# Spreading two rows with GpSimd instead of TensorE, zero matmuls among the first transposes, and a reordered end of the first stage in a fused RWKV-5 and SiLU kernel

## The chip, the cores and the metric

The kernel runs on one core of one Trainium2 chip. The metric is the device time of one launch, in microseconds (us); the figure quoted for a kernel is the median of several runs. Every time below comes from those runs or from one execution taken by the hardware profiler.

The engines are called as in the profile: PE is TensorE's matmul row and PEld its weight loads, DVE is VectorE, ACT is ScalarE, POOL is GpSimd, SP is SyncE. DMA transfers are issued from the queues of SP, ACT and POOL.

## The reference

A linear attention with a decaying state is followed by a two-layer network with SiLU. There are 4 batches, 8 heads, 768 time steps and a head size of 48; the second part has 3072 tokens of width 384 and a hidden width of 2048. All inputs and the output are float32.

```python
for t in range(S):
    cur = np.einsum('bhd,bhe->bhde', u[None] * kt, vt)
    y[:, :, t] = np.einsum('bhd,bhde->bhe', rt, state + cur)
    state = w[None, :, :, None] * state + np.einsum('bhd,bhe->bhde', kt, vt)
x = y.transpose(0, 2, 1, 3).reshape(B * S, H * D)
h = x @ w_in
out = (h * (1.0 / (1.0 + np.exp(-h)))) @ w_out
```

Here kt, vt and rt are the rows of k, v and r at time t; w (8 by 48) is the decay of each head and channel, and u (8 by 48) is the bonus factor of the present step.

## The kernel before

**Tiling.** The 768 steps are cut into 6 chunks of 128 steps. A unit is one chunk of one batch, so there are 24 units, numbered so that units 0 to 3 are the first chunk of the four batches, 4 to 7 the second, and so on. Four units of one chunk make a tile of 512 tokens for the network.

**One unit.** Three loads bring r, k and v of the unit into `rin`, `kin` and `vin` (line 71, 192 KB each). TensorE transposes r and k (`turn_one`, line 244, and `turn_ring`, line 254); DVE multiplies the transposes by powers of w into `rT` and `kT` (`decay_one`, line 260). For two units at a time 64 small float32 matmuls form the products of k and r (`product_pair`, line 283); DVE masks them (`masked`, line 300), and ACT casts v (`cast_v`, line 236, with two more copies that swap halves for odd units) and, from unit 4 on, r (`cast_r`, line 279). `outputs_y` (line 305) multiplies the masked products by v, and from the second chunk on adds the state's part. The bonus is made apart: POOL forms k times u (`bonus_ku`, line 209), then times r (`bonus_rku`, line 213), DVE sums over each head (`bonus_sum`, line 222), POOL multiplies v by the sum (`bonus_v`, line 227). For units 0 to 3 a matmul adds that to y in PSUM (`add_bonus`, line 321). POOL also forms k times its decay to the chunk's end (`decayed_k`, line 218), which `outputs_s` (line 325) uses for the state. y goes through a transpose into `xT`, the network's input.

**The network.** `l1` (lines 401 to 419) is a piece of the first layer: six matmuls for two of the 16 hidden tiles, then a SiLU on ACT. `l2` (line 451) and, for the first tile, `front_mm` (line 426) are pieces of the second layer. The first tile accumulates its second layer in the two `att` PSUM tiles, which the attention uses too, and `front_store` (line 431) copies it out of there on ACT.

**Order.** The schedule is by hand: each engine and each queue runs its instructions in the order in which the program issues them. After the constants (lines 97 to 138) a string of words named `order` (line 515) is walked word by word and covers units 0 to 7. A word names a step and a unit: Tr0 and Tk0 are the transposes of r and k of unit 0, rT0 and kT0 their products with powers of w, A01 a pair's products, am0 a mask, Y0, V0 and S0 the matmuls of `outputs_y`, `add_bonus` and `outputs_s`, ku0, ru0, rd0 and vu0 the four bonus steps, kc0 the decayed k, v160 and r164 the casts, y160 and yT0 the way of y into xT0. lr1, lk1 and lv1 are loads, issued on SP. q0 to q3 and o0 to o3 are loads of the network's weights, issued on POOL. L and G are first-layer matmuls and their SiLU for the first tile, M2.3 is the last of the four pieces of batch 2 in the second layer, osb2 its copy and store, H0 a whole piece of the next tile's first layer. hold6 is a memset on POOL (line 152) that writes a part of `rin` of unit 6, so that the load lr6 can't start ahead of it. clear writes zeros into the `att` tiles by six matmuls of a zero operand (`zeros`, line 155). Then a loop (line 547) takes two units at a time from unit 6 on, and between its attention steps calls `fill`, which takes pieces of the network off a list.

**The two rows.** w and u are loaded as one row each on one partition. They are needed on all 128 partitions: u for ku, and the logarithm of w for `lamC`, which the kc steps use. A matmul with a column of ones does that (`spread_row`, line 178): word ub for u, copied from PSUM to `u_bc` on DVE by ubc, and word wb for w, from which ACT takes the logarithm at once (`ln_w`, line 185).

```python
def spread_row(name, row):
    spread[name] = ps.tile([128, HD], FP, name="bc", tag="moe", bufs=4)
    nc.tensor.matmul(spread[name], ones, row, start=True, stop=True)
```

## Time and profile before

| What | Value |
|---|---|
| Median of 3 runs | 196.67 us (196.13 to 197.16) |
| The profiled execution's own time | 195.64 us |
| Its span in the profile | 193.8 us |
| Around the span | 1.84 us |
| Mean granted TensorE clock | 0.974 |
| Busy: PE, PEld, DVE, ACT, POOL | 186.7, 142.5, 102.1, 110.1, 120.6 us |
| Read from and written to HBM | 20.45 and 4.72 MB |

The span runs from the first to the last instruction that the profiler recorded. A share of busy time is a mean over stages with different limits, so the page is read by stage: constants and first loads (to about 8 us), the attention of units 0 to 3 (to about 25), the string's remaining words (to about 53), and then a loop that repeats every 14.3 us.

### The profile page before, as it was taken

How to read it: one execution, taken by the hardware profiler on the slowest of the kernel's cores; microseconds unless marked ns; L12 is line 12 of the kernel's file. 1: busy time of each engine (PE TensorE's matmuls, PEld its weight loads, DVE VectorE, ACT ScalarE, POOL GpSimd, SP SyncE). 2: the span in 40 equal slices, each digit the busy share in tenths (PEclk: the TensorE clock that was granted, in tenths of full speed). 3: DMA queues.
4: the chain of work that ended last, by engine and by line, in shares of the span. 5: the costliest groups of instructions: out<-in, count | busy, mean ns of one | idle time of the engine just before them, and what ended most of it. 6: DMA issues, size and time to landing. Idle time of an engine off the chain costs nothing.

```text
span 193.8 us, 5942 instructions
## 1 busy us (share of the span) xinstructions
PE 186.7 (96%) x2476; PEld 142.5 (74%) x2476; DVE 102.1 (53%) x193; ACT 110.1 (57%) x208; POOL 120.6 (62%) x160
## 2 busy tenths in 40 slices
PE   7799999999798999999999999999999999999994
PEld 2578689756597688688688697697697697796873
DVE  6767776640654645646546556456466365262110
ACT  5266877703468557557557567457558458462540
POOL 8895996975895496496496595595694680300000
PEclk9756999999999999999999999999999999999999
DMA  5999899919961761952762952942953941202202
GB/s 101 222 213 209 136 159 189 163 38 212 233 180 39 156 177 41 185 143 44 157 173 44 180 148 42 206 123 46 181 147 62 188 123 41 81 4 44 81 0 81
DMA packets 90126, 24.17 MB, mean 125 GB/s; under 512 B 83314, under 2 KB 90100, under 8 KB 90100
## 3 DMA queue, kind: packets, MB, share of 16 engines
q1 hardware_dynamic: 84992, 20.39, 47.7%
q0 software_dynamic: 3712, 3.15, 11.0%
q8 instruction: 19, 0.31, 0.7%
q10 hardware_dynamic: 1396, 0.27, 0.7%
q14 instruction: 7, 0.06, 0.1%
HBM read 20.45 MB, written 4.72 MB: 130 GB/s over the span
## 4 chain that ended last, share of the span: by engine, by line
PE 92%; DMA 2%; ACT 2%; DVE 1%; SPq 1%; issue 1%
PE hps L406 32%; PE ops L439 26%; PE att L293 10%; PE att L428 5%; PE att L251 5%; PE tr L258 3%; PE yp L318 3%; DMA kin<-in_k_dram 2%; PE yp L313 2%; PE sp L334 2%; PE ops L464 1%; PE yp L322 1%; SPq L73 1%; PE bc L180 1%; DVE am L300 1%; ACT gT L414 1%
## 5 line engine op out<-in xcount | busy, mean ns | idle before, releaser
L414 ACT ACTIVATE gT<-hps 128x512 f16<-128x512 f32 x96 | 56.4, 597 | 43.5 <-PE hps L406 41.1
L406 PE MATMUL hps<-xT,win 128*128 128x256 f16 (+1 forms) x564 | 70.0, 275 | 0.6 <-DVE y L353 0.5
L406 PEld LDWEIGHTS <-win 128*128 128x128 f16 x564 | 53.2, 98 | 9.2 <-issue 0.9
L439 PE MATMUL ops<-wout,gT 128*128 128x384 f16 x304 | 52.4, 326 | 0.0
L439 PEld LDWEIGHTS <-gT 128*128 128x128 f16 x304 | 29.1, 98 | 18.1
L229 POOL TENSOR_TENSOR vu<-vin,rku 128x384 f32<-128x384 f32 x24 | 19.7, 829 | 32.0 <-DVE rku L224 28.7
L300 DVE TENSOR_TENSOR am<-att,maskM 128x1024 f16<-128x1024 f32 x12 | 14.7, 1224 | 35.5 <-PE att L293 35.5
L211 POOL TENSOR_TENSOR ku<-kin,u_bc 128x384 f32<-128x384 f32 x24 | 24.1, 1007 | 3.8 <-DMA kin<-in_k_dram 3.8
L215 POOL TENSOR_TENSOR rku_f<-rin,ku 128x384 f32<-128x384 f32 x24 | 24.0, 1001 | 1.3
L219 POOL TENSOR_TENSOR kc<-kin,lamC 128x384 f16<-128x384 f32 x24 | 24.0, 1004 | 0.1
L293 PE MATMUL att<-rT,kT 48*64 48x128 f32 (+1 forms) x768 | 20.7, 257 | 1.1 <-ACT osb L445 1.1
L293 PEld LDWEIGHTS att<-rT,kT 48*64 48x64 f32 x768 | 18.7, 140 | 3.9 <-issue 1.7
L353 DVE TENSOR_TENSOR y<-yp,vu 128x384 f16<-128x384 f32 x20 | 11.2, 558 | 16.1 <-PE yp L318 5.4
L266 DVE TENSOR_TENSOR rT<-att,lamR 112x512 f32<-112x512 f32 x20 | 13.7, 686 | 9.3 <-PE att L251 9.3
L445 ACT COPY osb<-ops 128x384 f32<-128x384 f32 x16 | 7.7, 478 | 17.9 <-PE ops L439 17.9
L238 ACT CAST v<-vin 128x384 f16<-128x384 f32 x24 | 11.3, 509 | 6.3 <-DMA vin<-in_v_dram 6.2
L300 DVE TENSOR_TENSOR am<-att,maskX 128x1024 f16<-128x1024 f32 x12 | 14.6, 1216 | 0.0
L345 POOL TENSOR_TENSOR sdec<-st,wCT 112x384 f32<-112x384 f32 x16 | 13.2, 826 | 1.6 <-DVE st L368 1.5
L266 DVE TENSOR_TENSOR kT<-att,lamK 112x512 f32<-112x512 f32 x20 | 13.5, 681 | 0.0
L364 DVE TENSOR_TENSOR st<-sp,sdec 48x192 f32<-48x192 f32 x32 | 11.2, 351 | 2.6 <-POOL kc L219 1.6
L373 POOL CAST stb<-st 112x384 f16<-112x384 f32 x16 | 8.1, 505 | 7.3 <-DVE st L364 7.1
L281 ACT CAST rT<-rT 112x512 f16<-112x512 f32 x20 | 12.4, 620 | 0.2
(80 smaller groups left out, 198.2 us busy)
## 6 DMA issues: line engine op xcount, KB each, us to landing
rin<-in_r_dram SPq DMA_DIRECT2D x24, 192.0 KB, 3.6
vin<-in_v_dram SPq DMA_DIRECT2D x24, 192.0 KB, 3.6
kin<-in_k_dram SPq DMA_DIRECT2D x23, 192.0 KB, 3.5
out_dram<-osb SPq DMA_DIRECT2D x23, 192.0 KB, 3.0
win<-in_moe_w_in_dram POOLq DMA_DIRECT2D x4, 384.0 KB, 6.1
wout<-in_moe_w_out_dram POOLq DMA_DIRECT2D x4, 384.0 KB, 8.7
xT<-y SPq DMA_TRANSPOSE x18, 2.3
kin<-in_k_dram ACTq DMA_DIRECT2D x1, 192.0 KB, 3.6
```

The source lines that it names most:

```text
L211: nc.gpsimd.tensor_tensor(out=L(i)["ku"], in0=kin[i % NIN][:, :, 0:D], in1=u_bc, op=ALU.mult)
L215: nc.gpsimd.tensor_tensor(out=L(i)["rku_f"], in0=rin[i % NIN][:, :, 0:D], in1=L(i)["ku"], op=ALU.mult)
L219: nc.gpsimd.tensor_tensor(out=kc[i % NIN][:, :, 0:D], in0=kin[i % NIN][:, :, 0:D], in1=lamC, op=ALU.mult)
L229: nc.gpsimd.tensor_tensor(out=L(i)["vu"], in0=vin[i % NIN], in1=L(i)["rku"].unsqueeze(2).broadcast_to([128, H, D]), op=ALU.mult)
L266: nc.vector.tensor_tensor(out=L(i)[key].rearrange("p g (y t) -> p y g t", y=2), in0=L(i)["t"][0:PR, :, x], in1=lam.rearrange("p g (y t) -> ...
L281: nc.scalar.copy(out=L(i)["rT16"], in_=L(i)["rT"])
L293: nc.tensor.matmul(a[e][o0:o0 + HC, j, p, c0:C], kT[r0:r0 + D, p, s0:s0 + HC], rT[r0:r0 + D, p, c0:C], start=True, stop=True)
L300: nc.vector.tensor_tensor(out=am.rearrange("p h g c -> p (h g) c"), in0=L(i)["a"].rearrange("p h g c -> p (h g) c"), in1=(maskX if crossed ...
L345: nc.gpsimd.tensor_tensor(out=L(i)["sdec"], in0=st[b], in1=wCT.unsqueeze(2).broadcast_to([PR, NP, PW]), op=ALU.mult)
L406: nc.tensor.matmul(hps[:, f, :], win[:, q, (ft + f) * 128:(ft + f + 1) * 128], xts[sc][:, q, b0:b0 + nb, :].rearrange("p b t -> p (b t)"), ...
L414: nc.scalar.activation(out=gts[sc][:, ft:ft + m, b0 * C:(b0 + nb) * C], in_=hpss[b0, ft], func=AF.Silu)
L439: nc.tensor.matmul(opss[b], gts[sc][:, ft, b * C:(b + 1) * C], wout[:, ft, :], start=(ft == 0), stop=(ft == NFT - 1))
```

## The change

Four things are edited. Words and names are those of the section on the kernel.

- u and w are spread by GpSimd's partition_broadcast, from the one-partition row straight into SBUF: u among the constants, between the memsets of `st` and those of `rin` and `kin`; w by a new word wbc, between q0 and vu0. The two matmuls, the column of ones and the DVE copy are gone.
- Zero matmuls of 512 columns are added: clear has eight instead of six, three words z write to the `att` tile that the next pair of transposes does not use, and zs writes twice to a PSUM tile of its own just ahead of A01. The transposes of k of unit 0 go ahead of those of r of unit 1.
- For units 6 and 7 the casts v166, r166, v167 and r167, which stood in the loop's first pass, become words ahead of M2.3 and M3.3, the last second-layer pieces; osb2 and osb3 stand ahead of H0; a second piece H1 stands ahead of A67 and is taken off the loop's list.
- hold6 goes from after M0.1 to before Y4. The loads that follow change order: lv7 and lv6 come ahead of those of units 8 and 9.

```diff
     for b in range(B):
         nc.gpsimd.memset(st[b], 0.0)
+    nc.gpsimd.partition_broadcast(u_bc.rearrange("p h d -> p (h d)"), u_row)
     for i in range(B, NIN):
         nc.gpsimd.memset(rin[i][:, :, D:64], 0.0)
...
     def clear():
-        for n in range(6):
+        for n in range(8):
             zeros(att[n % 4 // 2][:, n % 2, :])
...
-    def spread_row(name, row):
-        spread[name] = ps.tile([128, HD], FP, name="bc", tag="moe", bufs=4)
-        nc.tensor.matmul(spread[name], ones, row, start=True, stop=True)
-
-    def copy_u():
-        nc.vector.tensor_copy(out=u_bc.rearrange("p h d -> p (h d)"), in_=spread["u"])
+    def spread_w():
+        nc.gpsimd.partition_broadcast(w_bc, w_row)
+
+    def zero_behind():
+        zeros(att[(len(turns) + 1) % 2][:, 0, :])
+
+    def zero_ring():
+        zs = ps.tile([128, 512], FP, name="zs", tag="moe", bufs=4)
+        for _ in range(2):
+            zeros(zs)
...
-        clear lr1 lk1 lk2 lnw lk3 eK ub lv0 lv1 lamK lr2 mx lr3 Tr0 ubc Tr1 lr5 rT0
-        Tk0 ku0 lv5 Tk1 rT1 lr4 ku1 kT0 Tk2 lv3 lv2 kT1 ru0 lk4 kT2 A01 ku2 lk5 rd0
-        lv4 kcm ru1 v161 wb q0 am0 Tr2 v160 vu0 lnwb am1 Y0 ku3 lamC Tk3 Tr3 rT2 ru2
+        clear lr1 lk1 lnw lk2 eK lk3 lv0 lv1 lamK lr2 mx lr3 Tr0 rT0 lr5 z z Tk0 kT0
+        ku0 lv5 z Tr1 Tk1 rT1 kT1 lr4 ku1 Tk2 lv3 lv2 ru0 lk4 kT2 zs A01 ku2 lk5 rd0
+        lv4 kcm ru1 v161 q0 wbc am0 Tr2 v160 vu0 lnwb am1 Y0 ku3 lamC Tk3 Tr3 rT2 ru2
...
-        sd4 L4.13 G4.12 am4 G0.10 L0.8 ku5 G4.13 L4.15 kc5 G0.8 Y4 S4 G4.15 M2.0 st4
-        ru5 Y5 M1.0 stb4 rd5 S5 sd5 M0.0 M2.1 vu4 st5 M3.0 stb5 y164 M0.1 hold6 vu5
-        lr6 M1.1 lk7 y165 L4.14 lk6 M1.2 G4.14 lr7 yT4 lk8 M1.3 lv7 M0.2 lk9 ku7 M0.3
-        lv6 M2.2 lv9 osb0 ku6 lv8 M2.3 lr8 ru7 yT5 Tr6 Tk6 xT5 lr9 xT4 kc6 M3.1 rT6
-        osb1 osb2 Tr7 Tk7 rd7 kT6 vu7 M3.2 rT7 ru6 M3.3 kT7 H0 osb3 rd6 A67
+        sd4 L4.13 G4.12 am4 G0.10 L0.8 ku5 G4.13 L4.15 kc5 hold6 G0.8 Y4 S4 G4.15 M2.0
+        st4 ru5 Y5 M1.0 stb4 rd5 S5 sd5 M0.0 M2.1 vu4 st5 M3.0 stb5 y164 M0.1 vu5 lr6
+        M1.1 lk7 y165 L4.14 lk6 M1.2 G4.14 lr7 yT4 xT4 M1.3 lv7 lv6 M0.2 ku7 lr8 lk8
+        lv8 lr9 lk9 lv9 M0.3 osb0 osb1 ku6 M2.2 ru7 yT5 xT5 Tr6 rT6 Tk6 kT6 kc6 v166
+        M3.1 r166 M3.2 v167 rd7 vu7 ru6 Tr7 rT7 Tk7 kT7 r167 M2.3 M3.3 osb2 osb3 H0
+        rd6 H1 A67
...
-    fillers.extend(first(1, 0, 2) + second(1, 0))
+    fillers.extend(first(1, 0, 4) + second(1, 0))
...
-        if i > B + 2:
-            fill(4)
-        else:
-            for n in (i, i + 1):
-                cast_v(n)
-                cast_r(n)
-                fill(2)
+        fill(4)
```

## The prediction

> **What bounds the kernel now.** I read the page's busy rows, then the chain that ended last.

> ```profile
> PE 186.7 (96%) x2476; PEld 142.5 (74%) x2476; DVE 102.1 (53%) x193; ACT 110.1 (57%) x208; POOL 120.6 (62%) x160
> PEclk9756999999999999999999999999999999999999
> PE 92%; DMA 2%; ACT 2%; DVE 1%; SPq 1%; issue 1%
> ```

> TensorE bounds the whole. Its matmuls carry 92% of the chain, so after the start a gain can only come from matmuls run sooner or faster. The clock row shows the weak place: slices 1 to 3 (4.8 to 19 us) are below full clock. By windows of 1 us it falls in the window 7 to 8 (0.68), is 0.50 from 8 on, and is full again by 18. The chain in order of time says what this costs, and where else PE stands still:

> ```profile
> 3.26 4.05 DMA kin<-in_k_dram
> 7.36 1.10 PE tr L258 x4
> 8.46 3.39 PE att L293 x62
> 11.85 1.57 PE bc L180 x2
> ...
> 16.86 1.08 PE yp L322 x2
> ...
> 18.30 1.52 PE att L293 x64
> ...
> 52.25 0.47 issue
> 52.72 0.48 ACT osb L445
> ```

> The same pair's products take 3.39 us at 8.46 and 1.52 at 18.30. The spreading of w (L180) is 1.57 on the chain. At 52.25 the products of units 6 and 7 wait 1.0 for ACT's copy out of `att`.

> Then GpSimd's own timeline at the start, since the change puts work there:

> ```profile
> 0.80 0.20 POOL masks.py:197 MEMSET ident<- 128x128 f32 x1 [0.29 <-POOLq L609]
> 1.08 0.29 POOL masks.py:199 TENSOR_SCALAR_AFFINE_SELECT ident<-ident 128x128 f32<-128x128 f32 x1
> ...
> 2.46 1.49 POOL L135 MEMSET st<- 112x384 f32 x4
> ...
> 5.73 1.01 POOL L211 TENSOR_TENSOR ku<-kin,u_bc 128x384 f32<-128x384 f32 x1 [0.61 <-DMA kin<-in_k_dram]
> ...
> 10.51 0.93 POOL L84 DMA_DIRECT2D win<-in_moe_w_in_dram  x1
> 11.46 0.84 POOL L229 TENSOR_TENSOR vu<-vin,rku 128x384 f32<-128x384 f32 x1
> ...
> 18.12 2.40 POOL L229 TENSOR_TENSOR vu<-vin,rku 128x384 f32<-128x384 f32 x3 [2.00 <-DVE rku L224]
> ```

> POOL is idle 0.61 us once between 0.8 and 16.1, and 2.0 after that. What is put into it there is delay for vu0 (11.46) almost in full; vu0 is what V0 (PE, 16.86) adds.

> [...]

> **The change part by part.**

> *Broadcasts.* [...] Removed: two PE records of u (0.91, ahead of transposes that wait for loads: 0), DVE's copy (0.56: 0), and w's 1.57 on the chain.

> [...] four real exchanges in POOL's order. No trace here prices one. [...] a gain is excluded, since each is an added step. [...]

> Queued behind them is all of POOL, then DVE's rd0 (waits for ru0) with kcm, am0 and am1 behind it, then PE's Y0 and V0 and all after, then ACT's y160. Durations from the trace:
> - [...]
> - ku0, ku1, ru0, ku2, ru1 at 0.96 each to 22.4; q0 0.93 to 23.4.
> - [...] vu0 ends 36.7.
> - ku3, ru2, ru3, kc0 at 0.96, vu1 and vu2 at 0.8: vu2 ends 42.2, against 19.8 now.

> V2 on PE then ends near 42.9 instead of 22.2: **+20.7**. POOL itself is 22.4 late, and has 1 to 2 us of lead over PE later on (kc3 ends 28.35, S2 needs it from 29.77; DVE waits 1.59 for kc5's issue near 38). It keeps about half of the difference: +21.5. PE stands idle before V0, so it restarts at half clock: [...] +2.

> *Zeros.* Two more in clear [...] end at 4.9 where Tr0 starts at 4.80; three z and two zs are 0.2 to 0.4 each, in PE's waits for loads (idle 5.2 to 5.96 and 7.05 to 7.36). Their gain, a clock that holds, would be 3.39 - 1.52 = 1.9 on A01 and about as much on what follows. Together with w's 1.57 it is worth nothing here, because vu0 sets V0. Moving Tk0 ahead of Tr1: 0, both wait for loads.

> *End of the string.* osb3 is out before A67, with H0 and H1 (0.66 each) over it: -1.0. Casts of units 6 and 7 leave ACT's line in the loop, where SiLUs stand behind them and PE waits: from A67 to the next transposes PE takes 53.25 to 62.19, 8.94 us, against 68.54 to 76.49, 7.95, in the next pass: -1.0. H1 only moves a piece: 0.

> *hold6, loads.* hold6's memset at 41.46 moves behind kc5 (37.8). SP has stood 23.0 us before it, so lr6 and the eleven loads behind it start up to 3.7 us earlier against their work. POOL's wait for kin (3.15 at 45.71) shrinks; worth 0, since PE's chain is solid from 32.08 to 52.25. If that cover went, o3 (issued 34.23, 8.7 to landing) would share the DMA with those loads; M0.3 needs it near 47, 4 us later.

> **Sum**: +21.5 + 2 - 2 = +21.5. The profiled execution took 195.64 (span 193.8 and 1.84 around it): 217.1. The median of before lies 1.03 above its profiled run, so I state **218**.

> **The rivals.**

> *A, exchanges that cost nothing to speak of* (the other side: faster). [...] T4 can't start before kin4 lands (16.43 + 3.7 = 20.1 against 22.16 now, -2.0). So -1.7 at the start and -2 at the end: 193. The clock need not hold for this: w's 1.57 goes either way. [...] It decides from 1.3 us for an exchange down: the shift at V2 is the four of them less 3.1 [...], and at 5.1 in all it only eats the end's 2.

> *B, dearer exchanges.* [...] 10 us each: 4 x 4.05 more, 234.

> *C, one trip.* The second pair is absent or cheap [...]: 11.9 less, 206.

> **How the numbers follow.** Main case 0.60, A 0.30, B 0.06, C 0.04. The main case alone, exchanges of 3.5 to 8.5 us, gives 208 to 228. A has 0.30, too much to leave out, so the range goes from 192 to 228; B, a third of the part of A (190 to 196) and little of the main case lie outside. A difference of 0.5% (1 us) is what a measurement here can tell from none. Faster 0.29 (A), same 0.03 (exchanges near 1.3 us), slower 0.68.

> **What would show it.** Right: gaps of about 6 us on POOL ahead of the first broadcast, ku0, the second broadcast and vu0; vu0 near 36, V2 near 43; PE idle with a half clock between 10 and 40; A67 without a wait for osb; the loop at 14.3 us a pass as now. Wrong: vu0 before 15 (A), or one pair of gaps (C). If A67 still waits, the -2 is lost. If vu0 is late and V2 isn't, my reading of who waits for POOL is wrong.

## The result, and the profile after

The changed kernel takes 220.95 us (median of 4 runs, 220.57 to 221.26), the kernel before 196.91 us (median of 4, 196.13 to 198.04). The ratio is 1.1215, with a 95% interval of 1.1155 to 1.1275: **slower by 24 us**. Ratios here and below leave out executions more than 1.5% above the fastest of the same kernel, so that a ratio and the quotient of two medians can differ a little. The profiled execution took 221.08 us, its span is 219.4.

First the page of the changed kernel: busy times, the granted clock in 40 slices, and the shares of the chain that ended last.

```profile
span 219.4 us, 5954 instructions
PE 187.9 (86%) x2479; PEld 142.7 (65%) x2479; DVE 101.6 (46%) x191; ACT 109.7 (50%) x208; POOL 122.3 (56%) x162
PEclk9995555559999999999999999999999999999999
PE 80%; issue 13%; POOL 3%; DMA 2%; ACT 0%; ACTq 0%; POOLq 0%
```

TensorE's busy time is nearly what it was, and it fills 86% of the span instead of 96%. What grew on the chain is "issue", from 1% to 13% of the span, some 28 us in which an engine waits for nothing that the profile shows. Which engine that is, and what waits behind it, is in the waits of the first 90 us (columns: who waited for whom, us in total, times, the longest).

```profile
DVE rku L226 <- POOL rku_f L217: 27.7, 4, 14.9
ACT lnw_bc L188 <- POOL w_bc L177: 20.1, 1, 20.1
...
PE yp L324 <- POOL vu L231: 14.2, 1, 14.2
...
PE yp L320 <- DVE am L302: 11.6, 1, 11.6
...
POOL w_bc L177 <- issue: 7.4, 1, 7.4
POOL ku L213 <- issue: 7.0, 1, 7.0
POOL vu L231 <- issue: 6.9, 1, 6.9
POOL u_bc L135 <- issue: 5.9, 1, 5.9
```

The last four rows are the cause and the first four what it does. GpSimd stands still four times, once ahead of each of its two broadcasts and once ahead of the first multiply behind each. Its timeline puts them in order; the idle time before an instruction stands in brackets.

```profile
2.73 1.50 POOL L134 MEMSET st<- 112x384 f32 x4
10.12 0.68 POOL L135 PARTITION_BROADCAST u_bc<-u_row  x1 [5.89 <-issue]
...
11.66 0.31 POOL L138 MEMSET kin<- 128x128 f32 x1
19.01 1.95 POOL L213 TENSOR_TENSOR ku<-kin,u_bc 128x384 f32<-128x384 f32 x2 [7.04 <-issue]
...
23.77 1.06 POOL L84 DMA_DIRECT2D win<-in_moe_w_in_dram  x1
32.19 0.68 POOL L177 PARTITION_BROADCAST w_bc<-w_row  x1 [7.36 <-issue]
39.78 0.82 POOL L231 TENSOR_TENSOR vu<-vin,rku 128x384 f32<-128x384 f32 x1 [6.91 <-issue]
```

The gaps are 5.89, 7.04, 7.36 and 6.91, together 27.2 us; such a gap is what the prediction calls an exchange. The eight memsets between the first two gaps run without one, right behind the broadcast. vu0 begins at 39.78 where it began at 11.46, and V0 waits for it on PE 14.2 us. In the chain in order of time, what V0 to V2 then take:

```profile
32.96 6.83 issue
39.78 0.83 POOL vu L231
40.61 0.04 issue
40.66 1.65 PE yp L324 x2
...
42.94 2.77 PE att L295 x64
45.71 1.58 PE yp L324 x2
...
48.25 1.45 PE yp L324 x2
49.70 0.76 PE att L253 x16
...
79.18 1.31 PE hps L408 x12
80.49 1.50 PE att L295 x64
```

V2 ends at 49.70 against 22.23 before, 27.5 late. These matmuls run at half clock: the window 41 to 50 has a granted clock of 0.50 and a busy PE of 9.00 of 9.00. At the end of the string A67 starts at 80.49 straight behind H0 and H1, with no wait for the copies out of `att`. The whole is then 25.6 longer (219.4 - 193.8), so the end gives about 1.9 back.

### The profile page after: what moved, and what is told of

The parts are those of the page before. It is cut to its first block, busy times and chain, and to the rows that moved or that the text cites. A ratio compares the mean times of both kernels' runs of the same rounds, so it can differ in the third digit from the quotient of the medians.

```text
span 219.4 us, 5954 instructions
## 1 busy us (share of the span) xinstructions
PE 187.9 (86%) x2479; PEld 142.7 (65%) x2479; DVE 101.6 (46%) x191; ACT 109.7 (50%) x208; POOL 122.3 (56%) x162
## 3 DMA queue, kind: packets, MB, share of 16 engines
q1 hardware_dynamic: 84992, 20.39, 42.2%
q0 software_dynamic: 3712, 3.15, 9.9%
## 4 chain that ended last, share of the span: by engine, by line
PE 80%; issue 13%; POOL 3%; DMA 2%; ACT 0%; ACTq 0%; POOLq 0%
PE hps L408 29%; PE ops L441 23%; PE att L295 8%; PE att L430 5%; PE att L253 4%; PE yp L324 2%; PE yp L320 2%; DMA kin<-in_k_dram 2%; PE yp L315 2%; PE sp L336 2%; PE ops L466 1%; PE tr L260 1%; POOL ku L213 1%; PE yT L393 1%; POOL win L84 0%
## 5 line engine op out<-in xcount | busy, mean ns | idle before, releaser
L416 ACT ACTIVATE gT<-hps 128x512 f16<-128x512 f32 x96 | 56.7, 598 | 37.8 <-PE hps L408 34.7
L408 PE MATMUL hps<-xT,win 128*128 128x256 f16 (+1 forms) x564 | 68.3, 275 | 0.0
L441 PEld LDWEIGHTS <-gT 128*128 128x128 f16 x304 | 28.5, 98 | 17.9
L226 DVE TENSOR_REDUCE rku<-rku_f 128x8 f32<-128x384 f32 x24 | 12.4, 546 | 27.8 <-POOL rku_f L217 27.7
L320 PEld LDWEIGHTS <-am 128*128 128x128 f16 x192 | 10.4, 100 | 13.2 <-DVE am L302 12.0
L324 PE MATMUL yp<-vu,ident 128*128 128x384 f32 x8 | 5.8, 822 | 14.2 <-POOL vu L231 14.2
L320 PE MATMUL yp<-v,am 128*128 128x48 f16 x96 | 6.0, 190 | 11.6 <-DVE am L302 11.6
```

Source lines behind the costliest of these rows:

```text
L320: nc.tensor.matmul(L(i)["y"][:, h, :], L(i)["am"][:, j, p, :], L(i)["vy"][:, h, :], start=False, stop=(sc > 0 and j == 1))
L408: nc.tensor.matmul(hps[:, f, :], win[:, q, (ft + f) * 128:(ft + f + 1) * 128], xts[sc][:, q, b0:b0 + nb, :].rearrange("p b t -> p (b t)"), ...
L416: nc.scalar.activation(out=gts[sc][:, ft:ft + m, b0 * C:(b0 + nb) * C], in_=hpss[b0, ft], func=AF.Silu)
L441: nc.tensor.matmul(opss[b], gts[sc][:, ft, b * C:(b + 1) * C], wout[:, ft, :], start=(ft == 0), stop=(ft == NFT - 1))
```

## The experiments

Times are medians; a ratio is to the kernel before, with its 95% interval.

**e1_matmul: the change without its broadcasts.**

```diff
-    nc.gpsimd.partition_broadcast(u_bc.rearrange("p h d -> p (h d)"), u_row)
...
-        nc.gpsimd.partition_broadcast(w_bc, w_row)
...
+    def spread_row(name, row):
+        spread[name] = ps.tile([128, HD], FP, name="bc", tag="moe", bufs=4)
+        nc.tensor.matmul(spread[name], ones, row, start=True, stop=True)
```

> The changed kernel with u and w spread by matmuls as before; zeros, reordered end, hold6 and loads stay as changed. Theory [...]: no gap of 6 to 7 us on POOL, vu0 ends before 14 us, and the time falls under that of the kernel before, 192 to 195 us, since the end's 2 us and a clock that holds remain. Rival (zero matmuls or the reordered end bring the loss, the broadcasts little): still above 210. Rival (the end's gain is hidden anyway): 196 to 197.

194.22 us (193.44 to 197.72), ratio 0.9851 (0.9818 to 0.9884). POOL has no gap of that kind; vu0 runs from 12.12 to 12.96. The whole loss, and 2.7 us besides, goes with the two broadcasts. A01 takes 2.00 with zeros ahead of it, at a clock of 1.00 from 8 to 16. This kernel is faster than both. The execution in its profile took 195.72 and is one of its slower ones.

**e2_bcast: the broadcasts alone, in place of the matmuls of the kernel before.**

```diff
+    nc.gpsimd.partition_broadcast(u_bc.rearrange("p h d -> p (h d)"), u_row)
...
-        lv4 kcm ru1 v161 wb q0 am0 Tr2 v160 vu0 lnwb am1 Y0 ku3 lamC Tk3 Tr3 rT2 ru2
+        lv4 kcm ru1 v161 q0 wbc am0 Tr2 v160 vu0 lnwb am1 Y0 ku3 lamC Tk3 Tr3 rT2 ru2
```

> The kernel before with only the two GpSimd broadcasts put in, no zeros, old order. Theory: four gaps of 6 to 7.4 us on POOL, 27 us together, V2 about 27 late, no 2 us back at the end: 222 to 225 us. Rival (the broadcasts cost little of their own, the rest of the edit does): under 205.

222.59 us, ratio 1.1319 (1.1264 to 1.1374), with gaps of 6.01, 7.05, 7.43 and 7.61, together 28.1. The two broadcasts alone cost 25.7 us. The changed kernel, with the rest of the edit on top, is 1.6 below this (222.59 - 220.95). That is not clear of noise: the two intervals overlap, and the gaps in this profile are 0.9 longer.

**e3_together: both broadcasts in one place.**

```diff
     nc.gpsimd.partition_broadcast(u_bc.rearrange("p h d -> p (h d)"), u_row)
+    nc.gpsimd.partition_broadcast(w_bc, w_row)
...
-        lv4 kcm ru1 v161 q0 wbc am0 Tr2 v160 vu0 lnwb am1 Y0 ku3 lamC Tk3 Tr3 rT2 ru2
+        lv4 kcm ru1 v161 q0 am0 Tr2 v160 vu0 lnwb am1 Y0 ku3 lamC Tk3 Tr3 rT2 ru2
```

> The changed kernel with w's broadcast moved right behind u's, [...]. Theory [...]: two gaps instead of four, of 6 and 7 us; 14 us less than the changed kernel, 206 to 208. Rival (the gaps belong to the broadcast instruction itself, or to the row that it waits for): the second broadcast has its own gap, and the time stays above 213.

205.10 us, ratio 1.0419 (1.0384 to 1.0455): 15.9 less than the changed kernel. POOL's timeline:

```profile
10.20 0.68 POOL L135 PARTITION_BROADCAST u_bc<-u_row  x1 [5.98 <-DMA vin<-in_v_dram]
10.75 0.67 POOL L136 PARTITION_BROADCAST w_bc<-w_row  x1
...
19.58 1.95 POOL L211 TENSOR_TENSOR ku<-kin,u_bc 128x384 f32<-128x384 f32 x2 [6.99 <-issue]
```

The second broadcast follows the first without a gap, so here a gap belongs to the change into the broadcasts or out of them, and not to a broadcast or its row. The load of v that the first bracket names is not what the broadcast reads; it only ended last before it. The saving is a little more than the two gaps (14.3), and the clock can account for the rest: A23, begun at 28.91, takes 1.67 here and 2.84 in the changed kernel at half clock, so that here the clock is full from about 29.2 on, by estimate, ahead of V1 and V2. vu2 is the second of three multiplies on POOL, and V2 the last two matmuls of the chain:

```profile
30.09 2.39 POOL L229 TENSOR_TENSOR vu<-vin,rku 128x384 f32<-128x384 f32 x3
```

```profile
30.96 0.91 PE yp L322 x2
...
32.40 0.73 PE yp L322 x2
```

vu2 ends at about 31.7 and V2 at 33.1, 1.4 behind it. In the changed kernel, at half clock, V2 ends 3.7 behind vu2 (49.70 and about 46.0).

**e4_end: a broadcast where nothing is queued behind it.** Its result is used by nothing.

```diff
+    w_bc = cst.tile([128, HD], FP)
+    nc.gpsimd.partition_broadcast(w_bc, w_row)
     fill(len(fillers))
```

> The kernel before with one unused broadcast of w behind POOL's last work in the loop, where POOL has nothing queued behind it. Theory (an exchange costs only what is queued behind it on POOL): a gap of about 7 us on POOL late in the span, and the same time as before, 196 to 198. Rival (an exchange stops other engines or the DMA queues too): 3 us or more above it, with gaps on PE at the same place.

200.81 us, ratio 1.0201 (1.0169 to 1.0234). By the number the rival wins, by the trace neither does. POOL's timeline:

```profile
0.78 0.20 POOL masks.py:197 MEMSET ident<- 128x128 f32 x1 [0.29 <-POOLq L611]
8.41 0.28 POOL masks.py:199 TENSOR_SCALAR_AFFINE_SELECT ident<-ident 128x128 f32<-128x128 f32 x1 [7.43 <-issue]
...
170.97 1.62 POOL L229 TENSOR_TENSOR vu<-vin,rku 128x384 f32<-128x384 f32 x2 [6.34 <-DVE rku L224]
178.48 0.68 POOL L595 PARTITION_BROADCAST w_bc<-w_row  x1 [5.89 <-issue]
```

From 172.6 to 178.5, the late gap, PE is busy 5.90 of 5.90 us and DMA moves 36 GB/s: this exchange stopped neither PE nor the DMA queues. There is a second gap that I had not expected, 7.43 at the very start, ahead of the affine-select. If it is the way back from the broadcast at the end of the launch before, it is what the 4 us come from; the next run tests that.

**e9_back: the same with the way back in the same launch.**

```diff
     nc.gpsimd.partition_broadcast(w_bc, w_row)
+    back = cst.tile([128, 1], FP)
+    nc.gpsimd.iota(back, pattern=[[0, 1]], base=0, channel_multiplier=1,
+                   allow_small_or_imprecise_dtypes=True)
     fill(len(fillers))
```

> The late unused broadcast of the run above, [...] so that both exchanges lie behind POOL's last useful work [...]. Theory (the 4 us of the run above are the exchange back, paid by the next launch ahead of its first affine-select, where the trace has a gap of 7.4 us): no gap ahead of the affine-select, two gaps of 6 and 7 us at the end of POOL, and the time of before, 196 to 197.5. Rival (late exchanges cost time of their own): 199 or more.

196.86 us, ratio 0.9995 (0.9980 to 1.0010). The affine-select starts at 1.28, as in the changed kernel (1.30), and both gaps lie late:

```profile
174.91 0.68 POOL L595 PARTITION_BROADCAST w_bc<-w_row  x1 [5.90 <-issue]
182.63 0.14 POOL L597 IOTA back<- 128x1 f32 x1 [7.04 <-issue]
```

Two exchanges, 12.9 us of POOL, cost nothing here (ratio 0.9995), where POOL has nothing left to do, and the gap at the start is gone: it was the way back, paid by the next launch.

**e5_tail: the string's end alone, in the kernel before.** The edit is that of `order` from sd4 on, the list of pieces and the loop's first pass.

```diff
...
-        osb1 osb2 Tr7 Tk7 rd7 kT6 vu7 M3.2 rT7 ru6 M3.3 kT7 H0 osb3 rd6 A67
+        M3.1 r166 M3.2 v167 rd7 vu7 ru6 Tr7 rT7 Tk7 kT7 r167 M2.3 M3.3 osb2 osb3 H0
+        rd6 H1 A67
```

> The kernel before with only the string's end (units 4 to 7: casts, second-layer pieces, stores, hold6, loads, H1) as changed. Theory: A67 has no wait for osb, the first pass of the loop loses its waits for ACT, and the time is 2 us under before, 194.5 to 195.5. Rival (the loop takes it back in a later wait): within 0.5 us of before.

194.91 us, ratio 0.9893 (0.9863 to 0.9923): 1.75 less than before.

**e6_zeros: the zeros and the start's order alone, with matmuls for u and w.**

```diff
-        clear lr1 lk1 lk2 lnw lk3 eK ub lv0 lv1 lamK lr2 mx lr3 Tr0 ubc Tr1 lr5 rT0
...
+        clear lr1 lk1 lnw lk2 eK lk3 ub lv0 lv1 lamK lr2 mx lr3 Tr0 ubc rT0 lr5 z z Tk0 kT0
...
```

> The kernel before with the start of the changed one but matmuls for u and w: eight zeros in clear, z, zs, k of unit 0 ahead of r of unit 1; old end. Theory: the clock holds through A01, which takes under 2.2 us instead of 3.4, and 1 to 2 us are left at the end, 194.5 to 196, POOL's chain setting the rest. Rival (the zeros only take room, the clock falls as before): 196.5 to 198.

195.48 us, ratio 0.9935 (0.9918 to 0.9953): 1.2 less than before; the zeros and the order are not told apart. What these zeros do to the clock and to A01 is seen in e1, which has them too.

**e7_busy: PE kept busy while it waits for vu0.**

```diff
+    def keep_busy():
+        for _ in range(48):
+            zeros(att[0][:, 0, :])
...
-        V0 v165 kT3 Y1 ru3 rT3 silu rd1 A23 kc0 rd2 rd3 vu1 y160 v162 am2 vu2 V1 v163
+        kb V0 v165 kT3 Y1 ru3 rT3 silu rd1 A23 kc0 rd2 rd3 vu1 y160 v162 am2 vu2 V1 v163
```

> The changed kernel with 48 more zero matmuls of 512 columns on PE ahead of V0, in PE's wait of 14 us for vu0. Theory (3 to 4 us of the loss are matmuls at half clock after the wait, as V0 to V2 take 9.0 us there against 5.4 before): the clock is full when V0 starts, and the time falls by 3 to 4, to 217 to 218. Rival (POOL sets that stretch anyway): the clock is full and the time falls by less than 1.5.

220.70 us (219.02 to 221.19), against 220.95 of the changed kernel: no gain. V0 did start at full clock (0.91 instead of 1.65), but the clock fell again at about 42.7, as A23 began. The 48 zeros had not filled the wait: they ended at 38.43, and PE stood idle for 3.0 us before V0. Three stretches of this kernel, with the granted clock behind POOL's busy time:

```profile
40.00:43.00 3.00, 1.58 (x19) 1.12 (x23) 0.00 (x0) 0.63 (x2) 2.45 (x3) 0.95 0.00 0
43.00:46.00 3.00, 2.43 (x64) 2.24 (x56) 1.64 (x3) 1.69 (x4) 3.00 (x5) 0.50 0.03 8
46.00:49.00 3.00, 2.94 (x15) 1.95 (x16) 1.83 (x2) 0.48 (x1) 2.96 (x5) 0.50 0.00 0
```

A23 took 2.80, as without the zeros (2.84). So neither theory was tested: the clock was not held over the stretch that was to gain. The four gaps of this execution are also 0.8 longer together than the changed kernel's (28.0 against 27.2), which could hide a gain of that size. POOL is busy 8.41 of these 9 us, so that a held clock can gain only what PE lies behind POOL; e3 gives an estimate of that, 3.7 - 1.4 = 2.3 us.

**e8_load: u and w spread by their loads.**

```diff
-        nc.gpsimd.partition_broadcast(w_bc, w_row)
...
+        nc.scalar.dma_start(out=dst, in_=bass.AP(tensor=src.tensor, offset=0, ap=[[0, 128], [1, HD]]))
```

> The changed kernel with u and w brought to all 128 partitions by the load itself (a source step of zero), neither broadcast nor matmul. Theory (spreading costs only by the engine that it blocks): no gap on POOL and 1.6 us of matmul less than e1 where PE waits for nothing else, 191 to 195, at or under e1. Rival (192 KB more in each of two loads delay the first k and r by 0.8 us each while the DMA share is over 1.0): 0.5 to 1.5 above e1.

The load of u moves behind that of k of unit 0, and wbc, now a load, ahead of lr3. 196.22 us, ratio 0.9983 (0.9967 to 0.9999), 2.0 above e1. The direction is the rival's, the size above its range. POOL's first multiply waits 2.03 us for the load of u and begins at 7.15 (6.36 in e1), and the chain waits until 17.96 for a load of r.

**e10_order: e1 with v of units 2 and 3 loaded ahead of unit 5's r and v.** With the exchanges gone, e1's chain at the start ends in ACT, behind a load of v:

```profile
10.90 7.12 DMA vin<-in_v_dram
18.04 0.52 ACT v L246
18.58 0.51 ACT vx L249
19.10 0.51 ACT vx L250
19.63 1.28 ACT L202
20.92 0.49 ACT y L359
```

This is v165, the cast of unit 5, which no one needs yet; y160, which PE's transposes wait for, stands behind it.

```diff
-        ... Tr0 ubc rT0 lr5 z z Tk0 kT0 ku0 lv5 z ... Tk2 lv3 lv2 ru0 ...
+        ... Tr0 ubc rT0 lv2 z z Tk0 kT0 ku0 lv3 z ... Tk2 lr5 lv5 ru0 ...
-        V0 v165 kT3 ... V1 v163
+        V0 kT3 ... V1 v163 v165
```

> The changed kernel with matmuls for u and w (as in the first run of this study), and the loads of v of units 2 and 3 ahead of those of unit 5, with unit 5's cast v165 behind v163. Theory (with the exchanges gone the start is held by ACT, which waits until 18.0 us for v of unit 5 while y160 and v162 stand behind it): that wait goes, and the time falls by 1 to 3 us more, to 191 to 193.5. Rival (the loads as a whole bound the start, whatever their order): 194 or more.

192.92 us (192.65 to 192.95), ratio 0.9796 (0.9776 to 0.9816): 1.3 under e1 and the fastest of all. y160 now begins at 16.57 instead of 20.92, and T4 on PE at 21.32 instead of 23.95. The order of the loads and the place of the cast were changed together, so which of the two does it is not shown. The chain at the start now waits for a load of k, until 22.7.

## Why the prediction was right

The main case came true: 218 was stated, 220.95 measured, with the cause that it named. By its steps:

**Four exchanges in POOL's order: right.** The prediction put about 6 us on each, which no trace of before showed. The way into the broadcasts took 5.89 (5.98 in e3, 6.01 in e2) and, right behind a DMA issue of POOL, 7.36; the way back took 7.04 and 6.91, and 6.91 to 7.61 over all runs. Four times 6 is 24.0, and 27.2 was measured; this is the sum's largest miss, +3.2.

**The broadcast.** It takes 0.68, measured at 10.12 and at 32.19. What the prediction counted for it was not shown by a trace either.

**The chain behind POOL: right.** vu0 was to end at 36.7 and ended at 40.6, vu2 at 42.2 and about 46.0 (the second of the three that begin at 44.40, 0.8 apart); the differences, 3.9 and 3.8, are the exchanges and broadcasts and 0.3 at POOL's start. DVE's sums, the masks, V0 and ACT's logarithm of w wait as listed.

**The restart at half clock: right in size.** PE had been idle for 14.2 us before V0, and V0 ran at 0.50. V2 was put 0.7 behind vu2, and 2 more for the clock; it ends 3.7 behind. e3, where the clock is full by then, has 1.4. So V2's own work behind vu2 was put 0.7 too small, and the half clock costs about 2.3, by this estimate. Such a stretch has no one length here. The clock is at 0.50 from V0's start at 40.66 to about 50.0, 9.4 us with PE busy throughout; in e3 half clock lasts 4.4 us from where PE's work begins again, at 24.8, by the estimate given there. In the kernel before it is at 0.50 from 7.36 to 17.60, with PE busy for 10.24 of these 10.24 us. What ends a stretch at half clock is not shown.

**POOL's later lead: not there.** The prediction gave POOL a lead of 1 to 2 us because "kc3 ends 28.35, S2 needs it from 29.77", and added 0.8 for what this would not cover. S2 takes kc2, which ended at 26.58, so the lead there was 3.2. At vu2 POOL is 26.3 late (46.0 against 19.75) and PE at V2 27.5, since its matmuls at half clock put it behind POOL; from V2 on the chain is all PE.

**The end: right.** The -2 measured 1.9 here and 1.75 alone (e5). Both of its halves are in the trace: V2 to A67 takes 30.8 us instead of 31.0 with H1 (0.66) put in, and A67 to the next transposes 7.94 instead of 8.94.

**The sum.** For the span 21.5 was forecast and 25.6 measured. Exchanges, broadcasts and POOL's start missed 3.9, V2's work and the clock 1.0 together, and the lead that was not needed took 0.8 off. That 218 lies nearer than this is in part luck: it has 1.0 added because the median of before lay that far above its profiled execution, while that of the changed kernel lies 0.1 below its own.

**Zeros: worth nothing under the broadcasts, right.** vu0 sets V0, as said. For the case without broadcasts the prediction had 1.9 on A01 and about as much on what follows. A01 does take 2.00 instead of 3.39, but zeros and order together bring only 1.2 us (e6).

**Rival A** fell with the four gaps. e1 comes nearest to its case and took 194.22, where it said 193. e1 is not quite that case, since it keeps the matmul that spreads w (0.91 on PE), and its three executions with the highest clock took 193.4 to 193.7. One step of the rival did fail: "T4 can't start before kin4 lands", 20.1 by its sum. vu1 began at 16.75 in e1's profile, but T4 at 23.95. The rival looked at POOL, PE and two loads, and not at ACT's line, where v165 waits until 18.04 for its load and y160 stands behind it. With that out of the way (e10) the time is 192.9.

**Rival B** fell: the longest exchange of all runs is 7.61, and these gaps do not follow the DMA traffic. The first lies in 4 to 10 us at a DMA share of 1.10, with 219 GB/s moving, and is 5.89; e4's late one, with 36 GB/s moving, is 5.89 too; the last of the changed kernel lies in stretches that move 0 GB/s and is 6.91. **Rival C** fell: the second pair costs no less than the first (14.3 against 12.9).

Not tried: hold6 and the loads by themselves, counted at nothing.

## What to carry to other kernels

In these runs a broadcast on GpSimd cost its own 0.68 us, a gap of 5.9 to 7.4 us ahead of it, and one of 6.9 to 7.6 on the way back, ahead of the next multiply, iota or affine-select; memsets and a second broadcast right behind the first had none. Look for gaps ahead of such an operation that are put down to "issue", or to a load that it does not read, and count everything queued behind. Gather them in one place (15.9 us here), or where GpSimd has nothing left to do, and put the way back there too (196.86 in e9 against 200.81 in e4). When a stall goes, ask every engine's line what it waits for next: here it was a cast that nobody needed yet.
